# A new order of all steps in a recurrence-and-MLP kernel that TensorE bounds

## The chip, the cores and the metric

One core of one Trainium2 chip runs the whole kernel. The metric is device time in microseconds, from the runs of one launch each; three runs of the kernel before gave 666.44, 667.33 and 671.19 us, median 667.33.

## The reference

Six inputs r, k, v, w, a, b of shape (4 batches, 8 heads, 768 time steps, 40 wide) go through a recurrence with a 40 by 40 state for each head. Its outputs, put side by side as a matrix x of 3072 rows by 320, go through a two-layer MLP with the exact gelu. The MLP's two weights arrive as 64-bit floats.

```python
for t in range(S):
    y[:, :, t] = np.einsum('bhd,bhde->bhe', rt, state)
    Sa = np.einsum('bhde,bhe->bhd', state, at)
    state_decay = state * wt[:, :, None, :] - np.einsum('bhd,bhe->bhde', Sa, bt)
    state = state_decay + np.einsum('bhd,bhe->bhde', vt, kt)
...
x = attn_out.transpose(0, 2, 1, 3).reshape(B * S, H * D)
h = x @ w_in
g = 0.5 * h * (1.0 + erf(h * inv_sqrt2))
return (g @ w_out).astype(np.float32)
```

## The kernel before

**Tiling.** The 768 time steps are cut into 12 chunks of 64, named 0 to 11. All 32 heads of a chunk are worked on together. Inside a chunk the recurrence becomes small matrix products (64 by 64 and 40 by 64, one for each head, 64 TensorE instructions to a group, each in one quadrant of the array), a triangular inverse, and one state handed to the next chunk. A chunk gives 256 rows of x, and these go through the MLP: one product to 2,048 columns (step `ph`), gelu, and one back to 320 (step `po`). These are big products; the ones above are the small groups.

**Steps.** The kernel is a set of Python generators, one for each kind of step and chunk. The ones that matter here, in the order in which a chunk needs them:
- `w`, `a`, `b`, `k`, `v`, `r`, `wq`, `bp`, `kp`, `vp`: loads, issued by SyncE (SP). `wi`, `wl`, `wo`: loads of pieces of the MLP's weights; `ci0` to `ci9` and `co0` to `co15` turn them from 64-bit to 32-bit floats on VectorE (DVE) and ScalarE (ACT) (L457 to L472).
- `logs` (L499, ACT): logarithm of the decays w. `sums`: their running sum on TensorE, then exponentials (L522, L525) on ACT.
- `wt` (chunks 3 on): the same decays in another layout: a transposition on DVE (L561), logarithm on ACT (L542), a scan on DVE (L544), two exponentials on ACT (L547, L549).
- `ta`, `tb`, `tk`, `tv`, `tr`: the other inputs transposed and scaled, by TensorE for chunks 0 to 2, by DVE for the rest (L561, then a multiplication in L588, L614 or L631).
- `N`, `A`, `RV`: products of these on TensorE (L149, where every small matmul is recorded), masked on DVE (L676). N goes out to memory and comes back to GpSimd (POOL) as `nb` (L784).
- `inv`: the inverse of 32 by 32 blocks, 31 rows one after the other on POOL (L792 to L801); it goes out to memory and is fetched again by `ft`. Chunk 0's inverse is made by repeated squaring on TensorE (`sq0`, `sq1`) instead, and put together by `cornerd0`, `placed`, `joinedd0`.
- `corner` (a DVE transposition L908 first, then TensorE and ACT L916) and `joined` (L931): the inverse of the whole 64 by 64 blocks.
- `av` (L760), `X` (L943), `sa`, `saT` (L980, L981), `M`: the small products that use them. `tn`: the state turned around (L997).
- `yy`, `qk`, `QY`: the last three groups of a chunk; their sums stand in two PSUM tiles until `y` (DVE L1045, into x) and `state` (DVE L1091, L1092) have read them.
- `ph`: 8 times 20 matmuls (L1119), gelu on ACT for every 40 (L1122).
- `po`: for chunks 0 and 1 a plain product (L1141). For chunks 2 on, Strassen's scheme: seven products of 16 matmuls, m1 to m7 (L1157), with sums of the operands on DVE ahead of them (s1 L1164, s2 L1172, and L1184 and L1185, here called b2) and of the results behind them (copies on ACT L1174, L1175, L1187; additions on DVE L1161), then stores by SP (L1131).
- `warm`: a filler matmul whose result nobody reads. `begin`: fillers at the very start.

**What sets the order.** One string, `ORDER`, holds 1,334 tokens. Each token names a step and a chunk, and runs that generator to its next `yield`. No engine reorders its instructions, so the string is at once the order of TensorE, DVE, ACT, POOL and SP. Numbers behind a colon are places: for TensorE's groups one of four PSUM tiles of two banks each (`duo0` to `duo3`), for others one of three scratch tiles in SBUF (`conv`). A group that takes a PSUM tile again waits until whoever read it last is done. The loop that reads the string stands at the end of the kernel:

```python
for token in ORDER.split():
    name, *at = token.split(":")
    places[:] = [int(x) for x in at]
    ...
    next(going[name], None)
```

For instance `po5` from its fourth token on puts its work into the engines' queues so: s2 on DVE, the copies of m1 and m2 on ACT, an addition on DVE, m5 (with a PSUM tile), m6, b2 on DVE, the copy of m5 on ACT, an addition on DVE, m3 (with a PSUM tile), m7, four additions on DVE, the store, m4 (with a PSUM tile), an addition, the second store.

Of the kernel before, what the change touches and what calls it, by code (L numbers as in the profile page):

```python
# [27 lines left out]
SECOND_PAIRS = (0, 2, 4, 6, 10)  # L28

ORDER = """  # L30
w0 begin6 pads1 consts0 w1 tails1 b1 inv1 zeros1 begin6:0 logs0 zeros2 wi0 gaps0 b0 consts0 logs1 tails0 pads0 a0
consts0 sums0:1 gaps1 sums0:2 zeros0 v0 sums0 zeros4 warm6:3 pads3 pads2 sums1:0 zeros3 shifts0 sums0 sc0 a1 sums1:3
sums1 tb0:2 sums1 sc1 wi0 ta0:1 r0 tb0 ta0 tb1:3 N0:0 N0 tb1 wi0 ta1:2 k0 ta1 N0 tv0:1 sq1 v1 tv0 sq0 N1:3 sq0 sq0:0
sq1 sq0 sq1:2 k1 sq0 sq1 warm1:1 N1 sq1 sk0 ci0:0 wi0 sq1:0 N1 ci0 sq1 tr0:1 sq1 ci0 tk0:2 wi0 tk0 sk1 wi0 sq0:3 sq1
sq0 tr0 A0:2 ci1:1 sq1:0 sq0 ci1 sq1 sq0 nb1 sq1 A0 sq1 wi0 sq0:1 wi0 sq0 RV0:3 sq0 RV0 sq0 wl1 sq1:0 wl1 sq1 inv1 r2
sq0:2 sq1 sq1 sq0 tk1:1 sq0 sq0 sq1:3 tk1 w2 sq1 sq0:0 sq0 cornerd0 placed2 av0:2 ci2:2 placed3 cornerd0:3 ci1 ci2
inv1 nb1 placed1 warm0:1 cornerd0 wl0 ci3:0 wl0 av0 av0:0 r1 ci2 joinedd0:1 av0 joinedd0 tr2:3 placed0 joinedd0 tr2
warm2:2 wi1 a2 ci3 sa0:0 sa0 sa0:1 inv1 sa0 b2 warm5:2 ci4:1 ci9:2 ci4 QY0:3:0 logs2 ci4 k2 qk0 warm7:2 ci9 y0 warm3:1
wi1 state0 wi1 A1:2 wi1 A1 wi1 sums2:1 wi1 inv1 ci9 wo2 sums2:0 sums2 ci3 tv1:3 tv1 tr1:2 sc2 sums2 tn1:0 ci5:1 tn1
ta2:3 ta2 ci5 av1:1 tr1 ci5 sk2 inv1 y0:0 tb2:3 wi1 inv2 ci7:2 tb2 wo6 zeros6 y0:2 ci7 zeros7 y0 y0 tk2:3 av1 ci6:0  # L40
N2:2 ci6 N2 ft1 tk2 co3:1 ph0:0 ft1 ci6 wi1 ph0 corner1:0 N2 ci7 X1:1 corner1:2 corner1 ft1 ph0 X1 ph0:3 wo0 ci8:0
co2:2 ci8 RV1:2 RV1 nb2 warm4:1 ci8 joined1:0 wo9 joined1 wq3 ph0 co0:0 joined1 co0 inv2 ph0 co0 v2 ph0:1 co2 co3
co1:0 sa1:2 co1 sa1 w3 co1 saT1:0 saT1 co3 ph0 co2 wo4 ph0 inv2 ph0:3 co6:0 wt3:1 co6 co7:2 ph0 vp3 co7 ph0 co7
yy1:2:0 logs3 M1:1 M1 tv2:3 wt3 co6 wo8 sums3:1 nb2 sums3 wt3 QY1 zeros5 a3 inv3 tv2 qk1 co4:2 y1 wo15 po0:1 inv2
co5:0 y1 state1 co5 co4 po0 co5 RV2:3 wo10 A2:0 co4 y1 tn2:2 A2 tn2 co9:0 po0 ta3 co9 wt3 inv2 co15:2 bp3 po0 co9 co15
av2:0 co11:1 kp3 co8:0 co11 av2 co11 ph1:2 co8 co8 wo14 inv2 ph1 co10:1 tb3 co10 ph1 wo13 ph1:0 co10 a4 ph1 RV2 ph1
inv4 ft2 co14:0 ph1:2 ta3 co14 wo12 ft2 co14 ft2 N3:3 co15 X2:0 k4 X2 ph1 corner2:1 co13:0 corner2:0 N3 corner2 co13
co12:2 N3 po0 co13 co12 joined2:0 tables0 joined2 k3 joined2 po0 ta4 ph1 co12 sa2:3 nb3 tables0 saT2:0 tk3:1 b3 sa2
sk3 saT2 po0 r3 inv3 yy2:2:3 po0 po0 M2:0 po0 nb3 M2 po0 tv3 ph1:1 inv3 po0 tr3 wq4 ph1 sc3 QY2 w4 qk2 y2 po1:0 state2
bp4 inv3 po1 logs4 b4 A3:2 y2 A3 X3:3 wt4:0 po1 wt4 v3 ph1 wt4 po1 y2 inv3 wt4 po1 po1 ta4 kp4 po1 inv3 vp4 av3:2 tb4  # L50
av3 sums4:1 po1 X3 po1 RV3:2 v4 ws0 sums4 N4:3 N4 inv5 sk4 RV3 ph2:1 N4 sc4 tk4:2 ph2 ft3 ph2 ft3 ph2:3 ws3 nb4 ws1
nb4 ph2 corner3:1 ph2 ft3 ph2:2 inv4 a5 corner3:1 corner3 w5 ph2 ph2 joined3:3 joined3 r4 tn3:1 joined3 tn3 inv4
saT3:3 saT3 sa3:2 sa3 logs5 po1 ph2:1 ta5 bp5 yy3:3:2 M3:0 M3 inv4 tv4 ph2 ph2 tr4 wq5 QY3 qk3 po2:0 po1 sums5:0 sums5
y3 po1 po2:1 state3 y3 po2 inv4 wt5:2 RV4:0 po2:1 po2 wt5 k5 A4:2 po2 A4 tn4:3 y3 tn4 wt5 po2:1 tables1 wt5 po2 po2
inv4 kp5 av4:2 tb5 av4 X4:3 po2 ph3:2 sk5 X4 a6 po2 ta5 ph3 v5 RV4 N5:3 N5 ws2 po2:1 N5 po2 ft4 po2 ph3 ft4 ph3:0 ft4
corner4:0 nb5 tk5:2 ph3 vp5 ph3 corner4:3 ta6 corner4 inv5 nb5 po2 po2:1 po2 joined4:2 joined4 joined4 ph3:0 b5 saT4:3
saT4 sa4:1 r5 inv5 sa4 ph3 ph3 sc5 ph3:2 w6 yy4:3:1 M4:0 M4 tv5 ph3 inv5 ph3 tr5 wq6 QY4 logs6 po3:1 qk4 bp6 state4
po3:0 kp6 y4 po3 po3:2 wt6:0 A5:2 po2 sums6:1 A5 wt6 inv6 k6 inv5 sums6 wt6 y4 po3 wt6 po3 po3:3 po3 po3 tn5:2 y4 tn5
av5:1 tb6 RV5:0 po3 av5 po3 po3:2 ta6 b6 po3 inv5 po3 a7 N6:1 X5:3 N6 X5 N6 sk6 ph4:2 RV5 tk6:1 ph4 ph4 ft5 ta7 ph4:1
ft5 sc6 ft5 A6:3 corner5:0 nb6 r6 inv6 po3 po3:0 po3 corner5:2 A6 corner5 ph4 joined5:0 joined5 ph4 joined5 ph4:2 vp6  # L60
sa5:3 sa5 saT5:0 saT5 inv6 ph4 nb6 ph4 yy5:1:3 w7 M5:0 tr6 tv6 ph4:2 M5 wq7 ph4 inv6 ph4 QY5 v6 logs7 po4:2 qk5 po3 y5
bp7 po4:0 wt7:1 state5 wt7 po4 kp7 po4:0 av6:2 inv7 av6 y5 inv6 wt7 po4 po4 po4:1 wt7 po4 po4 v7 sums7:3 X6:2 y5 po4
ta7 sums7 tb7 po4 po4:0 po4 a8 X6 N7:3 inv6 N7 RV6:1 tk7:2 N7 ph5:2 po4 k7 ph5 ph5 ph5:3 ft6 nb7 ph5 ft6 ph5 nb7
corner6:0 ph5:0 RV6 ft6 inv7 corner6:2 po4 corner6 tn6:3 r7 tn6 po4:1 po4 joined6:2 ta8 joined6 joined6 ph5 inv7 vp7
ph5 sa6:3 sa6 saT6:1 saT6 ph5:2 po4 yy6:0:3 bp8 M6:1 M6 inv7 tr7 ph5 ph5 tv7 QY6 po5:1 wq8 qk6 y6 po5:1 state6 y6 po5
po5:2 inv7 po5 wt8:0 A7:2 y6 RV7:0 A7 wt8 tn7:3 RV7 tn7 wt8 vp8 inv7 po5 po5:1 po5 wt8 po5 X7:2 av7:0 inv8 av7 tb8 sk7
kp8 po5 ta8 b7 inv9 po5 po5:3 po5 a9 po5 N8:0 N8 ft7 ph6:1 N8 ph6 ph6 ft7 ta9 ph6:3 ft7 corner7:1 X7 ph6 tk8:2 nb8 ph6
corner7:0 nb8 corner7 sc7 ph6:1 r8 inv8 joined7:2 joined7 joined7 po5 po5:3 po5 sa7:0 sa7 saT7:2 saT7 bp9 ph6 inv8 po5
ph6 ph6:3 w8 yy7:0:2 M7:1 M7 tv8 ph6 ph6 wq9 inv8 QY7 logs8 po6:0 qk7 tr8 v8 state7 po6:1 y7 v9 po6 wt9:1 tn8:3 y7 tn8
A8:0 inv8 A8 wt9 X8:2 sums8:3 po6:2 po6 sums8 wt9 y7 po6 po6:0 po6 wt9 po6 av8:1 av8 kp9 RV8:3 po6 tb9 b8 inv8 po6  # L70
po6:1 ta9 a10 po6 RV8 po6 k8 sc8 po6 po6:0 N9:3 po6 N9 X8 ph7:1 N9 tk9:0 sk8 ph7 po6 ph7 ft8 ph7:0 nb9 w9 ph7
corner8:1 ph7 ph7:3 inv9 ft8 ft8 A9:2 A9 corner8:1 nb9 corner8 vp9 ph7 ph7 inv9 ph7:0 logs9 joined8:1 joined8 r9
joined8 ph7 ph7 sa8:2 saT8:3 saT8 po7:2 k9 po7:1 sa8 inv9 ta10 yy8:0:3 M8:2 bp10 M8 tv9 po7 po7:0 po7 wq10 QY8 po7 qk8
y8 po7:2 state8 inv9 y8 po7 po7 po7 av9:1 y8 av9 sums9:0 po7 sums9 X9:3 wt10:1 tr9 po7:1 wt10 inv9 X9 tn9:2 kp10 wt10
po7 inv10 b9 po7 wt10 ph8:0 po7 inv11 ft9 ph8 sk9 tn9 ta10 ft9 ph8 tb10 ft9 ph8:3 corner9:2 ph8 a11 ph8 RV9:1 v10
N10:2 N10 sc9 ph8:0 N10 tk10:0 ph8 w10 corner9:3 corner9 po7:2 po7 ph8 joined9:3 nb10 joined9 r10 joined9 ph8:2 ta11
ph8 inv10 ph8 sa9:0 sa9 logs10 vp10 saT9:3 RV9 saT9 po8:1 po8:2 yy9:0:1 M9:3 k10 inv10 nb10 po8 po8:0 M9 po8 sums10:3
sums10 po8 tv10 QY9 wq11 qk9 y9 po8:2 state9 y9 po8 po8 inv10 X10:3 A10:0 po7 wt11:2 y9 A10 po8 wt11 po8 po8:1 po8 po8
inv10 po8 wt11 po8:0 av10:2 bp11 po8 wt11 tr10 ph9:1 kp11 ph9 ta11 inv10 ph9 po8 tb11 ph9:0 b10 av10 ph9 X10 sk10 ph9
N11:1 N11 RV10:2 tk11:1 N11 ph9:3 ft10 RV10 ph9 ft10 ph9 nb11 ph9:0 corner10:0 ft10 sc10 w11 ph9 inv11 ph9 corner10:1  # L80
corner10 po9:2 vp11 po9:2 joined10:3 joined10 joined10 po9 nb11 sa10:0 inv11 sa10 r11 saT10:1 po9:1 saT10 tn10:3 tn10
po9 po9 po9:0 yy10:1:3 v11 M10:2 M10 tv11 po9 inv11 po9 po9 logs11 QY10 qk10 y10 po9 po9:2 y10 state10 po9 po9 X11:0
y10 sums11:1 sums11 A11:3 A11 inv11 po9 po9:2 po9 tn11:1 tr11 tn11 av11:3 po9 av11 RV11:2 X11 b11 inv11 RV11 ph10:1
k11 ph10 ph10 sc11 ph10:3 sk11 ft11 ph10 ft11 ph10 ft11 ph10:0 corner11:0 ph10 ph10 corner11:2 corner11 ph10:1
joined11:3 joined11 joined11 ph10 ph10 saT11:0 saT11 po10:2 po10:2 yy11:3:1 M11:0 M11 po10 po10:1 po10 QY11 po10 qk11
y11 po10:0 y11 po10 po10 y11 po10 y11 po10 po10:2 y11 y11 y11 po10 y11 po10 po10 po10:1 po10 po10 ph11:3 ph11 ph11
ph11:0 ph11 ph11 ph11:2 ph11 ph11 ph11:1 ph11 ph11 po11:0 po11:3 po11 po11:2 po11 po11 po11:0 po11 po11 po11 po11
po11:2 po11 po11 po11 po11:1 po11 po11
"""


@with_exitstack
def kernel(
    ctx: ExitStack,
    tc: tile.TileContext,
    r: bass.AP,
    k: bass.AP,
# [1170 lines left out]
```

## Time and profile before

| what | us |
|---|---|
| runs, median (lowest to highest) | 667.33 (666.44 to 671.19) |
| span of the profiled execution | 661.8 |
| TensorE matmul busy in it | 646.7 |
| VectorE (DVE) busy | 416.0 |
| GpSimd (POOL) busy | 367.7 |
| ScalarE (ACT) busy | 239.3 |

The profiled execution has no run time of its own on record. Its span, from the first to the last instruction, is 5.5 us under the median of the runs.

In the lists of the profile each row names a line of the kernel, an engine, an operation, and the tiles it writes and reads. `PE` is TensorE's matmul, `PEld` its loading of weights, which runs beside it. A row of the waits reads "engine, line <- what ended the wait: us in total, times, longest us"; "issue" is time in which an engine waited for nothing that the profile shows. A timeline row has the start, the duration, the instruction, and in brackets the idle time before it and what ended it. Where TensorE's rows show many matmuls together, their ends are modelled.

### The profile page before, as it was taken

What the parts mean: (1) busy time and instruction counts of PE and PEld (TensorE: products, weight loads), DVE (VectorE), ACT (ScalarE), POOL (GpSimd) and SP (SyncE); (2) the same over time, 40 slices, a digit from 0 to 9 for tenths busy, and PEclk for the clock granted to TensorE, in tenths of its full rate; (3) what the DMA queues carried; (4) which work ended last, traced back from release to release, by engine and by line L of the source; (5) the groups of instructions that cost most, each with busy time, mean ns of one, the idle gap of its engine ahead of it and who ended that gap; (6) DMA issues with size and microseconds to landing.
All of it is one profiled execution on the core that took longest, in us unless ns stands there. A gap on an engine that the chain in (4) does not pass through costs nothing.

```text
span 661.8 us, 30753 instructions
## 1 busy us (share of the span) xinstructions
PE 646.7 (98%) x13768; PEld 567.3 (86%) x13768; DVE 416.0 (63%) x536; ACT 239.3 (36%) x305; POOL 367.7 (56%) x799
## 2 busy tenths in 40 slices
PE   8889999999999999999999999999999999999997
PEld 4777788777778988998998998998988999998987
DVE  1778989976483874983863963863765674632313
ACT  4355646432424622522522422515253242232020
POOL 6158536706857837846838836847823874840000
PEclk9999999999999999999999999999999999999999
DMA  9989675696676476764775485675685465450100
GB/s 136 164 192 176 158 167 132 153 159 146 116 132 134 105 137 134 140 116 112 145 141 107 94 153 124 119 147 110 115 146 111 103 121 102 86 101 3 42 1 21
DMA packets 300708, 79.41 MB, mean 120 GB/s; under 512 B 288584, under 2 KB 293328, under 8 KB 300576
## 3 DMA queue, kind: packets, MB, share of 16 engines
q1 hardware_dynamic: 299512, 74.92, 58.3%
q0 software_dynamic: 864, 2.36, 1.8%
q8 instruction: 108, 1.77, 1.1%
q14 instruction: 24, 0.20, 0.1%
q10 hardware_dynamic: 200, 0.16, 0.1%
HBM read 64.09 MB, written 9.70 MB: 112 GB/s over the span
## 4 chain that ended last, share of the span: by engine, by line
PE 82%; DVE 8%; SPq 5%; issue 2%; DMA 1%; ACT 0%; DVEq 0%; ACTq 0%
PE duo L1119 29%; PE duo L149 25%; PE duo L1157 22%; PE duo L1141 4%; PE duo L557 2%; SPq L213 2%; SPq L227 1%; DVE conv L466 1%; SPq L1076 1%; DVE conv L472 1%; DMA spare<-in_a_dram 1%; DVE conv L458 1%; DVE conv L457 1%; DVE aT L588 1%; DMA rows<-in_b_dram 0%
## 5 line engine op out<-in xcount | busy, mean ns | idle before, releaser
L1119 PE MATMUL duo<-xt,w_in_sb 64*128 64x256 f32 x1920 | 218.8, 381 | 1.4 <-issue 1.4
L1119 PEld LDWEIGHTS duo<-xt,w_in_sb 64*128 64x128 f32 x1920 | 182.5, 187 | 23.9 <-issue 2.3
L799 POOL TENSOR_TENSOR tmp<-W,Nb 128x56 f32<-128x56 f32 (+22 forms) x155 | 71.8, 464 | 79.9 <-DMA Nb<-N 51.4
L1122 ACT ACTIVATE gt<-duo 128x1024 f32<-128x1024 f32 x48 | 49.2, 1025 | 143.0 <-PE duo L1119 132.1
L799 POOL TENSOR_TENSOR tmp<-rT,Nb 128x56 f32<-128x56 f32 (+22 forms) x155 | 70.2, 453 | 52.8 <-DMA Nb<-N 41.0
L1157 PE MATMUL duo<-w_out_sb,gt 128*128 128x160 f32 x640 | 93.3, 303 | 0.0
L1157 PEld LDWEIGHTS duo<-w_out_sb,gt 128*128 128x128 f32 x640 | 87.6, 190 | 2.4 <-issue 0.8
L801 POOL TENSOR_TENSOR W<-W,tmp 128x56 f32<-128x56 f32 (+22 forms) x155 | 71.8, 463 | 12.1
L801 POOL TENSOR_TENSOR rT<-rT,tmp 128x56 f32<-128x56 f32 (+22 forms) x155 | 68.4, 441 | 12.1
L1157 PE MATMUL duo<-extra,conv 128*128 128x160 f32 x320 | 46.0, 301 | 0.0
L1157 PEld LDWEIGHTS duo<-extra,conv 128*128 128x128 f32 x320 | 43.8, 190 | 1.4 <-issue 0.5
L1141 PE MATMUL duo<-w_out_sb,gt 128*128 128x320 f32 x128 | 36.9, 440 | 0.1
L1161 DVE TENSOR_TENSOR os<-os,duo 128x160 f32<-128x160 f32 x40 | 12.7, 318 | 31.9 <-PE duo L1157 28.0
L1141 PEld LDWEIGHTS duo<-w_out_sb,gt 128*128 128x128 f32 x128 | 23.6, 190 | 10.1 <-issue 0.5
L1164 DVE TENSOR_TENSOR conv<-gt 128x1024 f32<-128x1024 f32 x10 | 12.7, 1266 | 27.5 <-ACT gt L1122 27.5
L605 POOL TENSOR_TENSOR rows<-rows,w_tile 128x640 f32<-128x640 f32 x9 | 15.8, 1761 | 25.0 <-DMA Nb<-N 16.0
L676 DVE TENSOR_TENSOR SM<-duo,left_upper 128x1024 f32<-128x1024 f32 x11 | 13.4, 1221 | 24.4 <-PE duo L149 24.4
L931 DVE COPY Tt<-duo 32x512 f32<-32x512 f32 x11 | 7.6, 689 | 30.4 <-ACT Tt L931 30.3
L149 PE MATMUL duo<-rT,late 40*64 40x64 f32 x1472 | 26.1, 219 | 0.0
L149 PEld LDWEIGHTS duo<-rT,late 40*64 40x64 f32 x1472 | 23.7, 135 | 2.1 <-issue 2.1
L1122 ACT ACT_TABLE_LOAD x14 | 18.0, 1283 | 19.1 <-DVE os L1161 14.7
L1157 PE MATMUL duo<-extra,gt 128*128 128x160 f32 x160 | 23.9, 302 | 0.0
(222 smaller groups left out, 1092.0 us busy)
## 6 DMA issues: line engine op xcount, KB each, us to landing
Nb<-N SPq DMA_DIRECT2D x40, 128.0 KB
VR<-in_v_dram SPq DMA_DIRECT2D x24, 160.0 KB
out_dram<-os SPq DMA_DIRECT2D x48, 80.0 KB
rows<-in_b_dram SPq DMA_DIRECT2D x22, 160.0 KB
rows<-in_k_dram SPq DMA_DIRECT2D x22, 160.0 KB
w_out_sb<-in_moe_w_out_dram SPq DMA_DIRECT2D x5, 640.0 KB
w_tile<-in_w_dram SPq DMA_DIRECT2D x36, 80.0 KB
Tt<-inv SPq DMA_DIRECT2D x44, 64.0 KB
```

What stands on the lines that cost most here:

```text
L149: nc.tensor.matmul(o, lhsT, rhs, start=first, stop=True, skip_group_check=True)
L213: nc.sync.dma_start(out=t[half(e)].rearrange("p g h d -> p (g h) d")[:, :, :D], in_=rows_of(src, c, e))
L557: nc.tensor.transpose(pt[:, g, n], src(g, n), ident)
L605: (nc.gpsimd if c in SCALED_BY_POOL or c >= NB else nc.vector).tensor_tensor(to, raws.pop((c, "k")), t["rw"], ALU.mult)
L676: nc.vector.tensor_tensor(to, pt, upper.unsqueeze(1).to_broadcast([P, NBL, C]), ALU.mult)
L799: eng.tensor_tensor(t, W[:, :nr, j:j + 1].to_broadcast([P, nr, rest]), Nb[:, j:j + 1, j + 1:].to_broadcast([P, nr, rest]), ALU.mult)
L801: eng.tensor_tensor(W[:, :nr, j + 1:], W[:, :nr, j + 1:], t, ALU.add)
L1119: nc.tensor.matmul(pt[:, x, s], w_in_sb[half(x), kt, p * P:(p + 1) * P], xt[half(x), kt], start=kt == 0, stop=kt == NK - 1)
L1122: nc.scalar.activation(gt[:, 4 * q:4 * q + 4].rearrange("p (x s) t -> p x s t", x=2), pt, ACT.Gelu)
L1141: nc.tensor.matmul(pt[:, g], gt[:, f, g * P:(g + 1) * P], w_out_sb[:, f], start=f == 0, stop=f == NF - 1)
L1157: nc.tensor.matmul(pt[:, n, :DM // 2], l_[:, f], r_[:, f], start=f == 0, stop=f == NF // 2 - 1)
L1161: nc.vector.tensor_tensor(to, one_, other, ALU.add)
```

## The change

Nothing but the string `ORDER` differs (lines 31 to 88). It holds the same 1,334 tokens' steps, each as often as before, in another sequence and with other places, so every engine gets the same instructions in another order. The groups of many small TensorE instructions stand at other points of its stream, among the big products of `ph` and `po`.

The diff replaces all lines of the string. Its first lines, and those around `state6`, `sums8` and the end:

```diff
-w0 begin6 pads1 consts0 w1 tails1 b1 inv1 zeros1 begin6:0 logs0 zeros2 wi0 gaps0 b0 consts0 logs1 tails0 pads0 a0
-consts0 sums0:1 gaps1 sums0:2 zeros0 v0 sums0 zeros4 warm6:3 pads3 pads2 sums1:0 zeros3 shifts0 sums0 sc0 a1 sums1:3
...
-ph5 sa6:3 sa6 saT6:1 saT6 ph5:2 po4 yy6:0:3 bp8 M6:1 M6 inv7 tr7 ph5 ph5 tv7 QY6 po5:1 wq8 qk6 y6 po5:1 state6 y6 po5
-po5:2 inv7 po5 wt8:0 A7:2 y6 RV7:0 A7 wt8 tn7:3 RV7 tn7 wt8 vp8 inv7 po5 po5:1 po5 wt8 po5 X7:2 av7:0 inv8 av7 tb8 sk7
-kp8 po5 ta8 b7 inv9 po5 po5:3 po5 a9 po5 N8:0 N8 ft7 ph6:1 N8 ph6 ph6 ft7 ta9 ph6:3 ft7 corner7:1 X7 ph6 tk8:2 nb8 ph6
...
-po5 ph6 ph6:3 w8 yy7:0:2 M7:1 M7 tv8 ph6 ph6 wq9 inv8 QY7 logs8 po6:0 qk7 tr8 v8 state7 po6:1 y7 v9 po6 wt9:1 tn8:3 y7 tn8
-A8:0 inv8 A8 wt9 X8:2 sums8:3 po6:2 po6 sums8 wt9 y7 po6 po6:0 po6 wt9 po6 av8:1 av8 kp9 RV8:3 po6 tb9 b8 inv8 po6
...
-po11:2 po11 po11 po11 po11:1 po11 po11
+consts0 w1 logs1 tails0 begin6 begin6:0 pads3 w0 logs0 sums1:0 warm1:1 b1 a0 sums1:1 sums1 sums0:2 sums0:3 b0 a1 sums0
+warm6:1 gaps0 ta0:1 sc1 k0 wi0 pads1 warm4:3 sums1 sums0 pads0 sc0 tb0:0 tails1 tb0 tb1:2 pads2 ta1:3 ta0 N0:0 shifts0
...
+tk7:1 b7 RV6:0 ft6 N7:2 N7 N7 ph5:1 ph5 corner6:1 ph5 ph5:2 sc6 ph5 ft6 corner6:1 RV6 corner6 X6:0 ft6 sk6 po4 v7
+joined6:1 ph5 ph5:2 ph5 ph5 nb7 inv7 joined6 ph5:3 X6 joined6 saT6:1 ta8 A7:2 A7 ph5 sa6:2 vp7 sa6 inv7 saT6 M6:1 tv7
+ph5 r7 yy6:3:0 k7 tr7 nb7 w7 M6 inv7 logs7 wq8 bp8 po5:1 po5:2 po5 po5:0 po5 po5 av7:1 sums7:2 QY6 qk6 kp8 av7 po5:1
+po5 po5 po4 wt8:0 y6 k8 wt8 wt8 state6 y6 inv7 po5 wt8 tb8 po5 po5:3 y6 a9 tn7:0 po5 sums7 ta8 sc7 inv7 po5 N8:1 N8
...
+saT7 w8 ph6 yy7:1:0 ph6 b8 M7:2 po6:1 po6:3 po6 M7 QY7 tr8 po6:0 tv8 wq9 bp9 qk7 po6 po6 po6:3 inv8 po6 po6 state7 po6
+b9 y7 av8:0 inv8 logs8 sums8:1 y7 wt9:0 wt9 wt9 av8 sums8 y7 inv8 RV8:2 RV8 po6 wt9 po6:0 po6 tb9 ta9 kp9 po6 ft8 po6
...
+ph11 ph11 ph11:2 ph11 po10 ph11 po11:0 po11:1 po11 po11:1 po11 po11 po11:2 po11 po11 po11 po11 po11:1 po11 po11 po11
+po11:2 po11 po11 warm5:1
```

## The prediction

> **What bounds the kernel now.** I read the busy shares first. The span is 661.8 us, and TensorE is busy in all but its last slice:
>
> ```profile
> PE 646.7 (98%) x13768; PEld 567.3 (86%) x13768; DVE 416.0 (63%) x536; ACT 239.3 (36%) x305; POOL 367.7 (56%) x799
> ...
> PE   8889999999999999999999999999999999999997
> ...
> DVE  1778989976483874983863963863765674632313
> ...
> PEclk9999999999999999999999999999999999999999
> ...
> q8 instruction: 108, 1.77, 1.1%
> ```
>
> So the time is TensorE's own work plus its pauses. DVE is the second to look at: 63% on average, but 7 to 9 tenths in the first quarter. Then TensorE's waits:
>
> ```profile
> PE duo L149 <- issue: 2.7, 4, 1.1
> PE duo L149 <- DVE w_in_sb L1220: 1.5, 1, 1.5
> PE duo L1119 <- issue: 1.4, 1, 1.4
> PE duo L149 <- ACT w_in_sb L871: 1.4, 2, 1.0
> PE duo L149 <- DVE aT L588: 1.2, 3, 0.6
> ```
>
> The largest rows are "issue": stops in mid-group with no semaphore, 4.1 us in five places, all before 143 us. By the timeline TensorE waits for nothing worth a row after some 160 us. By stretches of 20 us (PE, PEld, DVE, ACT, POOL busy; clock; DMA share; GB/s):
>
> ```profile
> 60.00:80.00 20.00, 18.95 (x403) 14.42 (x399) 18.72 (x27) 11.97 (x15) 14.39 (x28) 1.00 0.80 185
> ...
> 100.00:120.00 20.00, 20.00 (x497) 16.94 (x494) 19.29 (x34) 10.77 (x14) 13.96 (x31) 1.00 0.52 134
> 120.00:140.00 20.00, 19.65 (x325) 16.29 (x320) 19.76 (x38) 9.91 (x13) 10.01 (x26) 1.00 0.86 183
> ...
> 400.00:420.00 20.00, 20.00 (x489) 18.32 (x488) 10.00 (x14) 5.58 (x7) 16.62 (x41) 1.00 0.68 133
> ```
>
> Between 60 and 140 us both TensorE and DVE are full (DVE 75 of 80 us, with the conversions of the weights). Later TensorE alone is full. There DVE has half its time free, but it runs in order, so what counts is where in its queue the step stands that TensorE needs next. One such place in the present order, DVE's timeline around chunk 6:
>
> ```profile
> 367.38 1.29 DVE L1045 TENSOR_TENSOR xt<-duo,wpT 128x512 f32<-128x512 f32 x2 [0.52 <-PE duo L149]
> 368.58 0.48 DVE L1091 TENSOR_TENSOR st<-duo,st 128x320 f32<-128x320 f32 x1
> 369.10 0.49 DVE L1092 TENSOR_TENSOR st<-st,wpT 128x320 f32<-128x320 f32 x1
> 369.51 0.48 DVE L1091 TENSOR_TENSOR st<-duo,st 128x320 f32<-128x320 f32 x1
> 370.03 0.65 DVE L1092 TENSOR_TENSOR st<-st,wpT 128x320 f32<-128x320 f32 x1
> ...
> 375.47 2.28 DVE L544 TENSOR_TENSOR_SCAN conv<-going_on,conv 128x1024 f32<-128x1024 uint8 x1
> ```
>
> The reader is to see that y and state 6 are read out of PSUM within 3.3 us, and that the scan of the next decay comes 5 us later.
>
> **The change part by part.** No instruction is added or taken away: the 1,334 steps are the same, so the sums by engine stay. Only order and buffer places move.
>
> *TensorE's own work.* A run of big groups pays once per run: 20 matmuls of ph take 2.36 us alone, 40 take 4.52, 100 take 10.99, so 2.16 per 20 and 0.2 per run; Strassen's 16 and 32 (2.37, 4.54) say the same. A small group of 64 takes 0.95 to 0.98 before another small one and 1.04 to 1.13 before a big one. The present order has 174 runs (89 big, 85 small), the new one 156: 18 fewer at about 0.17, so 3.0 us less. One filler group (0.95) goes to the very end, beside the last additions. Together -4.0 us.
>
> *The spacing.* Counted through the new order, the small groups are not further apart. The shortest time in which 192 small-group matmuls pass (after the first ph) is 3.45 us now and 2.44 then; 384 pass in 10.33 and 9.86. There are some 14 places with 192 or more in a row (corner6, X6, joined6 is one), and none now above 144.
>
> *The start (to corner2, 144.5 us).* SP issues w1, a0, a1 and b1 earlier and the weights' pieces later, chunk 0's inverse has fewer conversions in between, and POOL begins inverse 1 some 5 us sooner. By the rows chunk 0's corner then comes at 41 us (47.5 now), and the first ph at about 72 (81.0). But the conversions are only put off: ahead of corner2's transposition DVE has 119 us of work in the new order and 117 in the present one, and TensorE 131 against 129. So DVE holds TensorE between ph0 and corner2. I wrote down both orders engine by engine with the rows' durations, 0.2 us from each release to its user (m7's product of po5 ends at 385.9, its first addition starts at 386.0 to 386.1), and marked every step that finds its input late. To corner2 the present order gives 7.8 us of pauses so (11.7 in the trace, the rest being "issue" stops), the new one 13.8: 1.6 in the first squaring, 1.6 av1 after y0's reading, 0.75 and 1.2 in ph0, 2.0 joined1, 1.0 tv2, 2.3 corner2, the rest small. That is +6.0; of the 4 us of "issue" stops I let half vanish behind these waits, -2.0. Bounds: -6 (the earlier start survives) to +6.
>
> *The later chunks.* The same marking finds 1.2 us of late inputs after corner2 in the present order, which the trace has nearly none of, and 13.4 in the new one. Of the latter I drop 1.2 in steps under 0.25, and keep five kinds, 12.2:
> - state behind other DVE work, 4.7 in five places. In full, chunk 6: in the new order DVE has y6, wt8's scan, then state6, and the Strassen product m3 of po5 takes a PSUM tile that state6 reads. After qk6 DVE needs 1.29 + 2.28 + 2.1 = 5.7 and two hops, 6.1 us; TensorE has only m5 and m6 between, 4.54. It stops 1.6. (Others: X4 0.6, po4's m5 0.7, po7's m3 0.8, po8's m4 0.9.)
> - the tile of m7 taken again before its four additions are done, 2.9: A5 1.2 (behind tb5's and tk5's four operations of 1.23 on DVE), X8 0.45, tn10 0.45, tn11 0.75.
> - Strassen's b2 (2.6 us) behind a scan, 1.6: po3 0.4, po4 1.2.
> - sums8, 1.7: logs8 stands on ACT behind po6's copy L1187, which starts when m6 ends (329.59 after 329.55 in po4's). Copy 0.30, table load 1.28, logarithm 0.74, two hops: 2.7; TensorE has one group, 0.95, in between.
> - N9 to N11 waiting for ta's multiplication, 1.4.
> Bounds: 0 (each is under 1.7 us, and a third of a microsecond more cover each would end half of them) to 14.
>
> [...]
>
> *POOL and the queues.* From N to the corner that needs its inverse TensorE has 57.9 to 66.5 us of work in the new order, 55.6 to 64.6 now, where POOL needs 33 to 36 and two transfers; I cost it at nothing. If the cover were gone, the corner would wait whatever is lacking. SP's issues after chunk 3 stand as far ahead of their users as now, by the same marking.
>
> *Sum.* TensorE now ends at 657.6. 657.6 - 4.0 + 6.0 - 2.0 + 12.2 = 669.8; the last addition and store take 4.2 more, as now: span 674.0. The median of the runs is 5.5 above the span (667.33 to 661.8), so 679.5; I say 679, as one hop less in the 0.4 us of every stop would take off about half a microsecond.
>
> **Rivals.**
> - *DVE keeps up, faster.* The earlier start survives and the late steps hide. It is decided at DVE's corner2 transposition: if that runs before 138 us, the conversions did not hold TensorE. For it: each late stop is short, and DVE is half free in every later stretch. Against: DVE is full from 60 to 140 us with the same work. 667.3 - 4.0 - 6.0 = 657.
> - *The two halve: no change.* Half the late inputs hide, and half the loss at the start: 667.3 - 4.0 + 2.0 + 6.0 = 671.
> - *The instruction stream runs dry, slower still.* The "issue" stops are 0.8 us on average (4.1 in five) and lie where many small matmuls follow each other; q8's 108 packets carry 16 KB each. With 14 places of 192 or more, none to all could stop: 0 to 11.5 us, half is 6, so 685. Against it: nothing of the kind after 143 us, though 128 pass in 1.76 us there. I take zero in the sum, since 144 in a row run without a stop now. [...]
> - *The change does not do what it says.* By the counts above it does not space the groups; then only the order of the other engines is left, which is the forecast.
>
> **How the numbers follow.** Forecast (late inputs on DVE and ACT) 0.55; no change 0.20; faster 0.13; dry stream 0.12. A measurement here can tell about 1%: faster is below 660.7, slower above 674.0. Faster 0.13; within 1% 0.22 (the no-change case and a little of the forecast); slower 0.65. The forecast's own range is 673 to 685. To leave out no more than 2 in 10 the range reaches down to 662, through the no-change case, and up to 688, half of the dry stream's.
>
> **What would show it.** Right: TensorE's waits show rows of DVE L1092, L1161, L1185, ACT L499 and DVE L588 after 200 us, together about 12; chunk 0's corner comes near 41 us but corner2 not before 146; TensorE is busy some 4 us less. A span under 662 with no such rows would make the mechanism wrong, and "issue" rows of more than 8 us would make it the dry stream.

## The result and the profile after

| what | before | changed |
|---|---|---|
| runs, median (lowest to highest), us | 667.84 (666.44 to 671.19) | 688.35 (685.95 to 691.94) |
| span of the profiled execution, us | 661.8 | 687.3 |

The changed kernel is slower: the ratio is 1.0308, with a 95% interval from 1.0264 to 1.0351. The sign was forecast; the size was not: 679 was forecast, and the time lies just above the range (662 to 688). The spans differ by 25.5 us, the medians by only 20.5. Wherever both are on record an execution takes some 1.7 to 2.1 us more than its span, so the profiled execution of the kernel before took some 664 us, less than any of its four runs in the table. What follows explains the 25.5 between the two profiles.

The page of the changed kernel, the lines that answer to those shown of the kernel before:

```profile
PE 653.6 (95%) x13768; PEld 575.1 (84%) x13768; DVE 409.0 (60%) x536; ACT 238.8 (35%) x306; POOL 362.1 (53%) x799
...
PE   9889998999999999899999689999999999999998
...
DVE  1667899994739934844955373682674674532403
...
PEclk9999999999999999999999999999999999999999
```

TensorE has a dent, a 6, in the 23rd slice, near 385 us. Its busy time did not fall, it rose by 6.9 us. The clock's row hides the reason, since a tenth is too coarse: the mean clock is 0.999 before and 0.990 now. The two profiles cut at corner2 (columns: window, length, busy time of PE, PEld, DVE, ACT and POOL, clock, DMA share, GB/s), first before, then changed:

```profile
0.00:144.50 144.50, 134.63 (x2908) 107.72 (x2908) 115.62 (x192) 70.39 (x92) 76.94 (x193) 1.00 0.84 163
144.50:661.80 517.30, 512.05 (x10865) 459.60 (x10864) 300.34 (x344) 168.92 (x213) 290.76 (x606) 1.00 0.55 108
```

```profile
0.00:148.90 148.90, 138.11 (x2914) 110.38 (x2914) 112.74 (x193) 71.40 (x94) 74.43 (x193) 0.99 0.80 151
148.90:687.30 538.40, 515.51 (x10859) 464.75 (x10858) 296.24 (x343) 167.45 (x213) 287.62 (x606) 0.99 0.56 106
```

Of the 25.5 us, 4.4 arise up to corner2 and 21.1 behind it. Up to corner2 TensorE's idle time is 9.9 against 10.8; behind it, 5.3 against 22.9. So 18.5 us are idle time, nearly all late, and 6.9 us are matmuls that took longer. TensorE's waits in the changed kernel:

```profile
PE duo L1157 <- DVE st L1091: 6.0, 2, 5.1
PE duo L149 <- issue: 5.2, 6, 1.5
PE duo L149 <- ACT os L1175: 3.6, 1, 3.6
PE duo L149 <- DVE st L1091: 1.9, 1, 1.9
PE duo L557 <- DVE xt L1045: 1.9, 1, 1.9
...
PE duo L149 <- ACT w_tile L499: 1.4, 1, 1.4
PE duo L149 <- DVE nT L614: 1.3, 2, 0.9
PE duo L149 <- DVE os L1161: 1.3, 1, 1.3
```

Of the rows that were forecast for the time after 200 us, state's is there (6.0, under L1091 and not L1092), the additions' (L1161, 1.3) and logs8's (L499, 1.4), 8.7 us of some 12; L1185 and L588 have none. The 1.9 of L149 behind L1091 lies at 118 us. "issue" is hardly above before. Two single stops stand out, 3.6 and 5.1 us. Both lie at the end of chunk 6. TensorE's timeline there:

```profile
378.38 1.14 PE L149 MATMUL duo<-VR,nT 64*64 64x40 f32 x64
383.12 0.77 PE L149 MATMUL duo<-w_tile,cum_m 64*64 64x320 f32 x8 [3.60 <-ACT os L1175]
383.71 2.56 PE L149 MATMUL duo<-SM,rows 64*64 64x104 f32 x64
386.02 2.38 PE L149 MATMUL duo<-VR,rows 64*64 64x104 f32 x64
388.33 4.61 PE L1157 MATMUL duo<-extra,conv 128*128 128x160 f32 x32
398.08 3.98 PE L1157 MATMUL duo<-w_out_sb,gt 128*128 128x160 f32 x16 [5.14 <-DVE st L1091]
```

The two groups behind the first stop (QY6 and qk6) take 2.56 and 2.38 us, where they take 1.66 and 1.61 in the kernel before; the product behind the second takes 3.98, where 16 matmuls alone take some 2.4. The clock by microseconds (window, length, PE busy, clock, DMA share, GB/s) tells why:

```profile
383.00:384.00 1.00, 0.88 (x24) 1.00 1.31 197
384.00:385.00 1.00, 1.00 (x38) 0.59 1.39 188
385.00:386.00 1.00, 1.00 (x32) 0.50 1.43 184
386.00:387.00 1.00, 1.00 (x32) 0.50 1.35 213
387.00:388.00 1.00, 1.00 (x40) 0.70 0.25 68
388.00:389.00 1.00, 1.00 (x25) 1.00 0.08 15
```

After this stop the granted clock is 0.50 for 3.41 us, and the two groups that run in it take 0.90 and 0.77 us longer than in the kernel before. That is 1.67 together, half of the stretch, so I count 1.7 us for each such stretch. Four such stretches lie in the changed kernel (at 50, 241, 384 and 398 us), none in the kernel before until its last matmul: 6.8 us, nearly the whole rise of the busy time. This holds for the two profiled executions. By the mean clocks of all executions on record, the four of the changed kernel lose 5 to 12 us (clock 0.982 to 0.993), those of the kernel before 0 to 3.3 (0.995 to 1.000).

What held ACT at the first stop:

```profile
371.05 1.02 ACT L1122 ACTIVATE gt<-duo 128x1024 f32<-128x1024 f32 x1 [2.27 <-PE duo L1119]
380.66 1.28 ACT L499 ACT_TABLE_LOAD   x1 [8.59 <-DMA w_tile<-in_w_dram]
381.96 0.74 ACT L499 ACTIVATE w_tile<-w_tile 128x640 f32<-128x640 f32 x1
382.60 0.27 ACT L1174 COPY os<-duo 128x160 f32<-128x160 f32 x1
382.77 0.29 ACT L1175 COPY os<-duo 128x160 f32<-128x160 f32 x1
```

logs7 waits 8.6 us for the load w7, and the two copies that free sums7's PSUM tile stand behind it. In the changed string w7 stands three tokens ahead of logs7, in the one before twelve; SP issues it from 374.0 us, when ACT has been free since 372.1. And what held DVE at the second:

```profile
392.98 1.25 DVE L561 STREAM_TRANSPOSE conv<-v_pairs 128x1024 f32<-128x1024 f32 x1 [6.60 <-PE duo L1157]
394.15 1.25 DVE L1045 TENSOR_TENSOR xt<-duo,wpT 128x512 f32<-128x512 f32 x2
395.35 2.29 DVE L544 TENSOR_TENSOR_SCAN conv<-going_on,conv 128x1024 f32<-128x1024 uint8 x1
397.56 0.47 DVE L1091 TENSOR_TENSOR st<-duo,st 128x320 f32<-128x320 f32 x1
```

wt8's transposition waits for m6, though m6 gives it nothing: it writes scratch tile 0, which holds m6's operand s2. y6, the scan and state6 stand behind it, and m3 needs the tile that state6 reads.

### The profile page after: what moved, and what is told of

Read it like the earlier page. It is cut to its first block, busy times and chain, and to the rows that moved or that the text cites. A ratio compares the mean times of both kernels' runs of the same rounds, so it can differ in the third digit from the quotient of the medians.

```text
span 687.3 us, 30768 instructions
## 1 busy us (share of the span) xinstructions
PE 653.6 (95%) x13768; PEld 575.1 (84%) x13768; DVE 409.0 (60%) x536; ACT 238.8 (35%) x306; POOL 362.1 (53%) x799
## 4 chain that ended last, share of the span: by engine, by line
PE 57%; SPq 15%; DVE 11%; POOL 5%; DMA 5%; issue 4%; ACT 2%; DVEq 0%; POOLq 0%; ACTq 0%
PE duo L1157 18%; PE duo L149 18%; PE duo L1119 16%; PE duo L1141 4%; POOL tmp L799 3%; SPq L224 3%; SPq L213 2%; SPq L227 2%; SPq L715 2%; DMA r_pairs<-in_r_dram 2%; PE duo L557 2%; POOL W L801 2%; POOL rT L801 1%; DMA v_pairs<-in_w_dram 1%; DVE conv L561 1%
## 5 line engine op out<-in xcount | busy, mean ns | idle before, releaser
L799 POOL TENSOR_TENSOR tmp<-rT,Nb 128x56 f32<-128x56 f32 (+22 forms) x155 | 66.1, 427 | 77.1 <-DMA Nb<-N 65.3
L1157 PEld LDWEIGHTS duo<-w_out_sb,gt 128*128 128x128 f32 x640 | 89.2, 193 | 7.3 <-DVE st L1091 5.4
L801 POOL TENSOR_TENSOR rT<-rT,tmp 128x56 f32<-128x56 f32 (+22 forms) x155 | 70.8, 457 | 12.1
L801 POOL TENSOR_TENSOR W<-W,tmp 128x56 f32<-128x56 f32 (+22 forms) x155 | 70.4, 454 | 12.1
L1141 PEld LDWEIGHTS duo<-w_out_sb,gt 128*128 128x128 f32 x128 | 23.4, 190 | 10.2 <-issue 0.8
L908 DVE STREAM_TRANSPOSE conv<-Tt 128x512 f32<-128x512 f32 x11 | 7.8, 712 | 35.2 <-DMA Tt<-inv 35.2
L1161 DVE TENSOR_TENSOR os<-os,duo 128x160 f32<-128x160 f32 x40 | 12.5, 313 | 26.8 <-PE duo L1157 21.4
L149 PE MATMUL duo<-rT,late 40*64 40x64 f32 x1472 | 26.4, 220 | 1.7 <-issue 1.4
L149 PEld LDWEIGHTS duo<-rT,late 40*64 40x64 f32 x1472 | 23.9, 135 | 4.1 <-issue 3.8
L544 DVE TENSOR_TENSOR_SCAN conv<-going_on,conv 128x1024 f32<-128x1024 uint8 x9 | 21.3, 2371 | 3.2 <-ACT conv L542 3.2
```

The lines of the kernel that those rows point to most:

```text
L149: nc.tensor.matmul(o, lhsT, rhs, start=first, stop=True, skip_group_check=True)
L544: nc.vector.tensor_tensor_scan(plain(logs_of), going_on, plain(logs_of), 0.0, ALU.mult, ALU.add)
L799: eng.tensor_tensor(t, W[:, :nr, j:j + 1].to_broadcast([P, nr, rest]), Nb[:, j:j + 1, j + 1:].to_broadcast([P, nr, rest]), ALU.mult)
L801: eng.tensor_tensor(W[:, :nr, j + 1:], W[:, :nr, j + 1:], t, ALU.add)
L1141: nc.tensor.matmul(pt[:, g], gt[:, f, g * P:(g + 1) * P], w_out_sb[:, f], start=f == 0, stop=f == NF - 1)
L1157: nc.tensor.matmul(pt[:, n, :DM // 2], l_[:, f], r_[:, f], start=f == 0, stop=f == NF // 2 - 1)
```

## The experiments

Times are against the kernel before on the same chip, whose median was 664.8 to 666.7 in these series. The changed kernel was not run again in them, so a difference to it goes by the two ratios. The theory to be tested: the loss is a few stops of the new order's own making, each made dearer by the clock. The rivals: late loads on a full SP queue; the order on DVE alone; a start that leaves everything behind.

**One load earlier.** w7 is issued ahead of vp7, r7, k7 and nb7.

```diff
-vp7 sa6 ... r7 ... k7 ... nb7 w7
+w7 vp7 sa6 ... r7 ... k7 ... nb7
```

> The changed kernel with one load moved: SP issues w7 (the decays of chunk 7) ahead of vp7, r7, k7 and nb7's second half, so some 13 us sooner. My theory: of the 25.5 us that the span grew, 10 to 12 fall in one place, 379 to 402 us. There ACT stands at logs7, which waits for w7 (issued at 374, since SP is busy 90% of the time), with the copies of m1 and m2 behind it; sums7 wants their PSUM tile and TensorE stops 3.6 us, and by the granted clock runs at half speed for some 3 us after, 1.7 us more. By this theory the stop and the slow stretch go, and the time falls by about 5, to 683. Rival: SP is simply full, and what w7 gains r7, k7 and inverse 7 lose; then the time stays within 1 us of 688. Rival, the forecast's: only the order on DVE matters, no change.

Measured 683.72, ratio 1.0242 (1.0192 to 1.0291); the interval overlaps the changed kernel's. The stop at sums7 is gone in the trace, but its span is 687.1. m3 still stops 5.3, tn5 2.7, and other stretches at half speed came in (mean clock 0.985, 0.990 in the changed kernel). The mechanism of the first stop is shown; a gain of the whole is not.

**Another scratch tile.** wt8 to wt11 get tile 2, which nothing else uses by then.

```diff
-wt8:0 ... wt9:0 ... wt10:0 ... wt11:0
+wt8:2 ... wt9:2 ... wt10:2 ... wt11:2
```

> The changed kernel with the scratch tile of wt8 to wt11 changed from 0 to 2, which the new order does not use after 335 us; all orders as they are. My theory: wt8's transposition waits on DVE until m6 of po5 has read s2 out of tile 0 (6.6 us idle to 392.98), with y6, the scan and state6 behind it, so m3, whose PSUM tile state6 frees, stops 5.1 us and the clock is halved for another 3.5 us. With tile 2 the transposition runs when wq8 has landed, near 386, state6 ends near 394, and m3 stops about 1.3 with no slow clock: 5 to 6 less, 683. The forecast's theory (state 6 is late only since the scan stands ahead of it) expects no change. If the loads were the limit, wq8's landing, the gain is under 2.

Measured 680.92, ratio 1.0219 (1.0168 to 1.0271), some 6 us under the changed kernel by the ratios, as expected, though the two intervals just touch. In its trace the transposition runs at 384.56 and state6 ends at 391.3; m3 does not stop at all. The scan still stands ahead of state6 there, so the scan alone does not stop m3: the second stop came from the place number of a scratch tile, not from a late load.

**Both.**

> Both edits, the load of w7 earlier and wt8 to wt11 in tile 2. My theory: the two stops are separate, one behind the other, so the gains add, 10 to 11 less, about 677.5. If they are two faces of one late load, both together give hardly more than the better one alone, 682 or 683. The forecast's theory expects 688.

Measured 681.62, ratio 1.0215 (1.0168 to 1.0262): no more than the tile alone. By the trace ph6 comes 13.4 us sooner than in the changed kernel, but QY7 only 10.0, as with the tile alone: a stop of 1.7 us and a half clock at 413 us take the rest back. m3 stops 0.9 here. The gains did not add.

**State 6 first.** state6 moves ahead of wt8's transposition on DVE.

```diff
-wt8:0 y6 k8 wt8 wt8 state6
+state6 wt8:0 y6 k8 wt8 wt8
```

> The changed kernel with state6 moved ahead of wt8's transposition on DVE, so ahead of the scan and of the wait for the scratch tile; nothing else. My theory: state6 runs as soon as qk6 is done, m3 does not stop, and the slow clock after it goes too: 6 to 7 less, near 682. The forecast's theory counts 1.6 for this place: 686.5. A third: y6, which still waits behind the transposition, or the late loads, take the place of state6, and the stop only moves to the next group: no change.

Measured 686.1, ratio 1.0282 (1.0239 to 1.0324): less gain than my theory had; the interval covers the changed kernel's 1.0308, so no gain is shown. m3 still stopped 1.9, now behind y6 (which stayed behind the transposition), and the clock still halved after it (mean 0.992).

**SP relieved.** Half of the loads of r and v in pairs left out from chunk 5 on, so r and v are partly old data there; in the changed kernel, and in the one before as control.

```diff
-                    for e in range(2):
+                    for e in range(1 if c >= 5 else 2):
```

> The changed kernel with half of the loads of r and v in pairs left out from chunk 5 on (4 issues in place of 8 each; half of r and v in these chunks is then old data, every wait and every operation of the other engines stays). SP has some 10 us less to issue for each of seven chunks, out of about 45 in 50 us. Theory SP: in the new order the loads come late since SP, 90% busy, waits behind late steps and does not catch up; then w7 and the loads of r, wq, bp come earlier, sums7 does not stop (5 with its slow clock), and the small stops at tn5, N6 and A5 shrink: 680 or less, against 688 of the changed kernel. m3 of po5 still stops, for its scratch tile is no load. Theory DVE: the new order on DVE makes the stops by itself; then less than 2 us change.

> The same cut in the kernel before, as the control. SP is as busy there (514 us of issues in both), but TensorE waits for nothing after 160 us: both theories expect no change beyond 1 us, so 666 to 668. If it gets faster by several us, SP was a bound already, and the run above says nothing about the order.

Measured 679.88, ratio 1.0214 (1.0185 to 1.0243), and 662.21, ratio 0.9951 (0.9931 to 0.997). The changed kernel gains some 6 us by its ratio, the control some 3. In the changed one sums7 no longer stops, and m3 still does, 5.1 us. That would leave about 3 us for SP's lag beyond the control, which the intervals do not set apart from nothing; the stop that went is the one that w7 brought. The edit also takes the transfers away, so it does not tell SP's issues from the transfers. The control's 3 us were not expected, and its trace does not explain them: it is 2.9 us ahead of the kernel before by 160 us, where nothing was cut, and 1.2 at the end, and other executions of the same start lie as far ahead.

**y and state first in all chunks.** Right behind qk on DVE.

> The changed kernel with y and then state of chunks 2 to 10 moved on DVE to right behind qk, as in the order before, all else as it is. This undoes what the forecast blamed most. The forecast's theory: it counted 4.7 us of stops for state behind other DVE work, and y's loads and stores on SP would also be free sooner; 5 us less, 683. Theory with the scratch tile and the slow clock added: m3 of po5 alone stops 5.1 and costs 1.8 in clock, tn5 1.9 behind y4, so 8 to 10 less, 679. Theory SP: the loads stay late and the stops only move: under 2 us.

Measured 707.37, ratio 1.0628 (1.0588 to 1.0667): 20 us slower than the changed kernel, against every theory. TensorE's waits and the mean clock:

```profile
PE duo L1157 <- DVE gt L1184: 11.4, 4, 4.7
PE duo L149 <- DVE aT L588: 4.5, 2, 4.0
PE duo L149 <- ACT os L1175: 3.9, 1, 3.9
PE duo L1157 <- ACT os L1175: 3.8, 1, 3.8
```

```profile
core 0: 707.4 us, clock 0.969
```

DVE, which now waits for qk, keeps b2 (L1184, L1185) behind it, and m3 needs b2. By the changed order m5, m6 and m3 follow qk6 directly on TensorE; after qk8 it is one small group, m6 and m3, and after qk9 and qk10 m3 at once. In the order before other groups stand between: after qk6 come m1, m2, A7, RV7 and tn7, and only then m5. With the groups joined like this b2 (2.6 us) has to go ahead of y and state (3.4), so what I undid was needed, by this reading of the rows; a step that moves on one engine is only as good as the room that TensorE's order leaves. And (1 - 0.969) of 707 us, 22 us, are lost to the clock in this execution, 15 to 17 in the other three, against the 5 to 12 of the changed kernel.

**SP by due time.** From 165 us on, on top of both edits.

> The kernel with both edits (w7 earlier, wt8 to wt11 in tile 2; 681.6 us, 15 above before), and from 165 us on SP's queue in another order: at each point the issue whose user could run first, as the trace of that kernel tells; the other engines' orders are untouched. Theory SP: of the 44 us that TensorE loses there against its fastest pace, 26 come after 150 us (8 in the kernel before), and if these come from late loads, y transfers and inverses, half of them go: about 672. Theory DVE: the loads are late only because DVE frees their buffers late; within 2 us of 681.

Measured 704.47, ratio 1.0599 (1.0538 to 1.066). It does not decide between the two theories. The waits show that I had only moved the lateness: the inverses came back late for the corners.

```profile
PE duo L149 <- DVE conv L908: 15.0, 3, 8.2
PE duo L1157 <- DVE st L1091: 8.8, 3, 5.6
```

Its clock is 0.973, 19 us.

**The order in halves.** The order before up to a step, then the remaining steps in the changed order, or the reverse.

> The order before up to joined3 (some 210 us), and from there the changed order: the same steps, the changed start left out. In the changed kernel the lag behind the kernel before was 3.6 us at QY3 (220 us) and 25.5 at the end. Theory SP/DVE order of the later chunks: the loss lies in the later order itself, so about 22 of the 25 stay, 686 to 689 against some 667. Theory start: the late stops come from the start, which leaves SP and POOL behind for good; then most of the loss goes, 670 or less.

> The changed order up to the logarithm of chunk 7 (some 364 us), and from there the order before (sums7 in the PSUM tile that it has in the changed one). The changed kernel was 9.7 us behind at the first ph5 and 19 to 21 after the hand-over of chunk 6. If the loss of that hand-over belongs to TensorE's and DVE's order in it, this kernel keeps 6 to 10 of the 25.5: 673 to 677. If it comes from the lag that SP has by then, whatever stands behind, it stops all the same: 685.

> The changed order up to the Strassen steps after chunk 7's corner (some 430 us), and from there the order before. It holds the hand-over of chunk 6 in the changed order: 20 to 26 behind, 688 to 692. The difference to the run cut at 364 us is the price of that one stretch, 12 or more by my theory; by the theory of a lag on SP the two are alike.

> The order before up to joined8 (some 450 us), then the changed one. In the traces the changed kernel loses nothing from QY8 to the end (26.4 behind there, 25.5 at the end), though the stop at sums8, at 451 us in the changed kernel, lies before the cut. So 666 to 667, at best 1 us faster than before: fewer changes between groups should show here, if anywhere. If the late order loses by itself when its inputs come as late as in the changed kernel, 670 or more.

| kernel | median | ratio (interval) |
|---|---|---|
| before to 210 us, then changed | 683.63 | 1.0253 (1.0192 to 1.0315) |
| changed to 364 us, then before | 678.46 | 1.0206 (1.0161 to 1.025) |
| changed to 430 us, then before | 686.32 | 1.0313 (1.0273 to 1.0352) |
| before to 450 us, then changed | 667.87 | 1.0039 (1.0009 to 1.0069) |

The first lost some 3 us less than was expected, and the stretch between the second and the third 4 less. Most of the loss stays without the changed start, and the last third of the changed order costs 0.4%. The first kernel, whose start is that before, has the same two stops:

```profile
PE duo L1157 <- DVE st L1091: 5.1, 1, 5.1
PE duo L149 <- ACT os L1175: 3.0, 1, 3.0
```

So they belong to the changed order behind 210 us, not to what the start left behind. The stretch from 364 to 430 us is worth about 8 us, the difference of the second and third rows. In the second, sums7 still stops 5.0 for logs7, since the late load lies ahead of its cut. No version that holds part of the changed order beat the kernel before.

**Stops alone.** Six stops of three lengths in the kernel before, whose order is untouched, ahead of ph6 to ph11. The step, here the middle length (the short one has one multiplication over 128 columns, the long one five over 512):

```diff
+    @step
+    def stop(c):
+        pt = duo()
+        mm(pt[:, 0, :P], ident, ident)
+        some = pt.rearrange("p z n -> p (z n)")[:, :512] if 512 > 512 else pt[:, 0, :512]
+        for _ in range(2):
+            nc.vector.tensor_scalar(some, some, 1.0, None, ALU.mult)
+        mm(pt[:, 0, :P], ident, ident)
+        yield
```

> The kernel before with six short stops of TensorE put in, ahead of the first group of ph6 to ph11: a filler matmul of 128 columns into the PSUM tile that ph takes next, one DVE multiplication by 1.0 of it in place (128 columns), and a second filler over it, which has to wait for DVE. Nothing reads the results. A stop should be about 0.5 us where DVE is free, longer where its queue is not empty. Theory clock: half speed follows only when TensorE stands for about 1 us or more, so these cost themselves alone, 6 times 0.5 and 6 times 0.3 for the fillers, 4 to 6 us in all, and the granted clock stays 1.00. Rival: any stop brings it; then 6 times 1.7 more, 15 us.

> The same six stops with two DVE multiplications over 512 columns, some 0.6 us each: stops of about 1.6 us. Theory clock (a stop of 1 to 2 us is followed by stretches of 3.41 us at half speed, as at 241 us of the changed kernel): most of the six are followed by one, 1.7 us each, so 6 times 1.6 + 0.3 + 1.7 is 22; without the clock it would be 11. Rival, the half speed of the changed kernel has another cause (bursts of small matmuls, the power of these): no stretch at half speed, 11.

> The same six stops with five such multiplications, about 3.4 us each. Theory clock: every one is followed by one stretch of 3.41 us or two, so 6 times 3.4 + 0.3 + 1.7 to 3.4, 32 to 43; without the clock 22. If only stops above some 3 us bring it, this kernel shows the stretches and the one with middle stops does not.

Measured 682.2, 692.43 and 712.87 (ratios 1.0271, 1.0406 and 1.0704; intervals 1.0208 to 1.0335, 1.0347 to 1.0465, 1.0658 to 1.0749). The waits for the stops in the three, and the clocks:

```profile
PE duo L149 <- DVE duo L1224: 9.5, 6, 2.7
```

```profile
PE duo L149 <- DVE duo L1224: 15.4, 6, 3.0
```

```profile
PE duo L149 <- DVE duo L1224: 28.7, 6, 5.2
```

```profile
core 0: 676.1 us, clock 0.997
```

```profile
core 0: 689.4 us, clock 0.990
```

```profile
core 0: 712.4 us, clock 0.971
```

The stops are longer than planned (1.6, 2.6 and 4.8 us on average), since DVE's queue is not empty. Up to the last matmul the half clock holds for 3.4 us behind one of the six short stops, for 13.7 us behind three of the six middle ones, and for 6.8 us behind each of the six long ones. Half of that is lost: 1.7, 6.8 and 20.5 us (2.0, 6.9 and 20.7 by the mean clocks). With the stops that makes 11, 22 and 49 us; the spans grew by 14.3, 27.6 and 50.6, the fillers among them. So stops bring the half clock in an order whose profiled execution shows none without them. One execution of each does not show how the price grows with the length. By the mean clock the profiled one of the short stops loses 2 us, but the other three 6 to 11; the four with middle stops lose 7 to 12, the four with long ones 19 to 21.

## Why the prediction was wrong, step by step

- **The waits as the cause: right in kind.** The steps are the same (ACT has one table load more, 306 instructions against 305), and most of the loss is late inputs on DVE and ACT in the later chunks. The dry instruction stream did not come: "issue" is 5.2 us against 4.1.
- **TensorE's own work, -4.0: not seen.** Busy time rose by 6.9, of which the half clock makes 6.8, so next to nothing is left of the saving.
- **The start: the right number by luck.** corner2 comes at 148.9 (144.5 before, so +4.4 for the +4.0 of the sum), but only 0.9 of it is idle time; 1.7 is the clock at 50 us, the rest work that stands earlier. The first ph came at 78.3, not at 72 (81.0 before).
- **The late inputs, 12.2: idle time behind corner2 rose by 17.6.** Three forecast stops came at about their size: A5 1.3 (1.2), po4's m5 0.9 (0.7), sums8 1.4 (1.7). m3 of po5 stopped 5.1 (1.6) for another reason, below. The others did not come: X4, X8, tn10, tn11, b2 of po3 and po4, N9 to N11, po7's m3 and po8's m4. In their place stand stops that were not forecast, sums7 3.6, tn5 1.9 and N6 0.9 among them. At sums8 the load's own row held: it took 1.28 us from 449.09, and the logarithm began at 450.39, 0.02 us behind it. (The kernel before does have late inputs behind corner2, 0.6 at 207 us and 0.4 at 239, close to the 1.2 of the marking.)
- **The step that failed is the five kinds of late input.** It followed PSUM tiles from reader to next writer, but not the scratch tiles in SBUF. So it missed that wt8's transposition waits for m6; with the tile changed m3 did not stop, and with both edits it stopped 0.9, so this wait is most or all of m3's 5.1. The 1.6 that the sum had there was mis-sized: it counted all four operations of state6 (2.1), but m3 begins at 398.08, as the first one ends (397.56 and 0.47). With 0.5 in place of 2.1 DVE needs 4.4 us where TensorE has 4.54 of work, and by the sum's own terms no stop is left; that one came at this place is luck. The step also let SP's issues "stand as far ahead of their users as now". They did not: w7, moved to three tokens ahead of logs7, came 8.6 us late for ACT and cost 3.6. SP has 774 issues of 0.66 us, 515 of 662 us before, so it has little room to catch up.
- **A term was missing: the clock, 6.8.** The trace of before has no stretch at half speed until its last matmul, so the sum had no price for one, and the price could only come from the runs: 1.7 us for a stretch of 3.41. They also show that the length of a stop alone does not tell whether it brings one: in the kernel with short stops one of 1.60 us (at 542 us) was enough, while one of 2.72 (at 489) was not. The largest stop of the forecast, 2.3 us, lies between these two.
- **Where the terms go.** Against the forecast's +12.2 of span: +6.8 clock, +4.1 for the saving that did not come, +5.4 late idle time, -3.1 pauses at the start that did not come. That is 25.4, for 25.5 measured. It has to add up, since a span is idle time and work; what the experiments show by themselves are the two largest stops and the price of a stop in clock.

What stays open: why the gains of w7 and of the scratch tile do not add, and how much of the 2.2% that remain with the scratch tile changed (TensorE's order, or the loads) one could get back without changing TensorE's order; the two attempts to settle it on a larger scale changed more than they were meant to.

## What to carry to other kernels

When groups are joined to save changeovers, count for each join what the other engines must do between the last reader's release and the next use: here a join was to save 0.17 us by the rows, which did not show in the sum, and single stops of 3.6 and 5.1 us came from a late load and a scratch tile. Follow every tile that is written again, scratch as well as PSUM, and every load from its place in the queue to its user, above all where the queue is as full as SP's here (515 of 662 us). Give each forecast stop of TensorE from about 1.3 us on (the shortest that brought it here) a chance of a price for the clock (1.7 us for each stretch of 3.41) besides its own length.

## What the runs showed of the hardware that was not expected

- The granted clock falls to 0.50 in stretches of 3.41 us or twice that, behind stops that may be as short as 1.3 us (241 us in the changed kernel, with 0.4 shortly ahead of it). The length does not settle which stops bring it: 1.60 did and 2.72 did not in one execution, 2.74 did and 2.92 did not in another. In the kernel with long stops (3.7 to 5.2 us) every one brought 6.8 us of it.
- Where a stop falls counts as well. The four stretches of the changed kernel begin at 49.68, 240.83, 384.19 and 397.84 us, which is 56, 42 and 4 times 3.413 us apart (348.16 us in 102 steps, and one stretch is as long as a step), so in this execution they lie on one grid. Cut on such a grid, all 17 traces together have 32 windows at full clock in which TensorE was busy for less than 45% (in the changed kernel those from 380.77, 31%, and 394.43 us, 0%): the next window was at half clock behind every one of them. Of the 118 windows between 45 and 73% it was behind 18, and behind none above. The kernel with short stops has both cases (window, length, TensorE busy, clock, DMA share, GB/s). Its stop of 2.72 us lies across the first two windows, the one of 1.60 inside the third, and the fourth follows on the third:

```profile
484.12:487.53 3.41, 2.39 (x18) 1.00 0.66 138
487.53:490.95 3.42, 1.72 (x14) 1.00 0.90 156
...
538.73:542.14 3.41, 1.81 (x70) 1.00 0.55 123
542.15:545.55 3.40, 3.40 (x14) 0.50 0.94 184
```

What decides between 45 and 73% stays open: the second window had 50% and brought nothing, the third 53%.
- The same start has its corner2 at 142.0 us in one profiled execution (that of the order before up to 450 us) and at 144.5 in another (the kernel before), so it moves by 2.5 us by itself.
